# Clustered attention followed by a gated long convolution: TensorE's order written by hand, with routing and convolution units woven between attention steps

## The chip, the core and the metric

The kernel runs on one core of one Trainium2 chip. The metric is the device time of one execution in microseconds. Before the change the median of 2 runs is 709.45 us (708.78 to 710.13).

## The reference

```
q_assign = argmax(normalized q . normalized centroids)     # 16 clusters per head
k_assign = argmax(normalized k . normalized centroids)
scores = where(q_assign[q] == k_assign[k], q k^T / 8, -1e9)
attn = softmax(scores); x = attn v, heads side by side      # (4, 768, 512)
proj = x @ w_proj; x1, x2, x3 = the three 512-wide parts of proj
x2_conv = irfft(rfft(x2, axis=seq) * rfft(filter), axis=seq)
out = (x1 * x2_conv * x3) @ w_out
```

There are 4 batches, 8 heads, 768 positions, 64 channels a head; all inputs and the output are f32.

## The kernel before

The work is cut into eight *groups*, numbered from 0: four heads of one batch each, so that an even group and the odd one after it make a batch. A group has two *pairs* of heads, and a pair is worked off in six *steps*, one for each 128 keys.

`routing` (L248) finds the clusters of one group. Per pair and per Q or K it transposes six tiles on TensorE (L255), copies them out with ACT (L258), casts them with POOL into the operands `aug` (L260, L261) and multiplies with the normalised centroids (L264). The similarities are transposed back (L270), a chain on DVE (L274 to L282) makes one-hot rows, these are transposed (L286), scaled (`ohT`, L288) and written under Q and K in `aug` by eight DMAs on the SP queue (L293). So one matmul gives the score and the mask at once.

`attention` (L297) does one pair. A step has for each of the two heads two score matmuls in bf16 (L306) into a tile of two PSUM banks, an exp on ACT (L310) into one of eight f32 buffers `p`, and then four value matmuls in f32 (L314): for each half of the queries one for each head, the first head's into partitions 0 to 63 of the accumulator `o`, the second's into 64 to 127. DVE sums the exps into `acc` (L321). At the end of a pair, TensorE sums `acc` over the keys (four matmuls of 32 columns, L330); the denominators go through DRAM in a chain of DMAs on SP (`dd`, `dn`, `dr`, `rb`, L336 to L345); DVE scales the result (L348) and makes `uT` (L350, L351), POOL casts it to `xT` (L349).

`hyena` (L355) does the convolution of one batch after its two groups: the projection of x2 (L362), a transform along the sequence (`spectrum`, L230) with multiplications by the filter's spectrum (L370, L371), then for each of four *channel blocks* the projections x3 and x1 (L379), the inverse transform (L393) and the product (L402), and last the output projection (L409) and the store. `tables` (L156) makes the transform's matrices `fw` (L167 to L188), their transposes `inv` (L196, L199) and the filter's spectrum `hm` once at the start.

PSUM has eight banks: three tiles of two banks (`wide()`, L61) that scores, routing, convolution and tables share, and the accumulator `o` with two. The order of every engine's instructions comes from the language's scheduler, which goes by the program's order as a priority and by its own estimate of when an instruction is ready. The main loop (L425) traces the loads and the routing of group n+1, then attention of group n, then for odd groups the convolution.

Of the kernel before, what the change touches and what calls it, by code (L numbers as in the profile page):

```python
# [30 lines left out]
def kernel(  # L31
# [25 lines left out]
    psS = ctx.enter_context(tc.tile_pool(name="psS", bufs=3, space=PSUM))  # L57
    psO = ctx.enter_context(tc.tile_pool(name="psO", bufs=1, space=PSUM))
    dram = ctx.enter_context(tc.tile_pool(name="dram", bufs=2, space=bass.MemoryType.DRAM))

    def wide(nm="ps"):  # L61
        return psS.tile([128, 2, 512], F32, name="ps")
# [3 lines left out]
    vraw = ctx.enter_context(tc.tile_pool(name="vraw", bufs=2))  # L66

    def load_qk(b, g):
        qk = [[None] * 2 for _ in range(2)]
        for pr in range(2):  # L70
            for j, src in enumerate((q, k)):
                tl = qk[pr][j] = raw.tile([128, NT, 2, D], F32, name="qkraw")
                for hp in range(2):
                    nc.sync.dma_start(tl[:, :, hp], src[b, 4 * g + 2 * pr + hp].rearrange("(p t) d -> p t d", t=NT))
        return qk

    def load_v(b, g):
        vv = vraw.tile([128, 4, 384], F32, name="vraw")
        nc.sync.dma_start(vv, v[b, 4 * g:4 * g + 4].rearrange("h (p t) d -> p h (t d)", t=NT))
        return vv  # L80

    qk_raws = {(0, 0): load_qk(0, 0)}
    v_raws = {}

# [6 lines left out]
    nc.gpsimd.memset(ones32, 1.0)  # L91

# [11 lines left out]
    cbd = consts.tile([128, 4, 32], F32)  # L104
    nc.gpsimd.memset(cbd, 0.0)
    with tc.tile_pool(name="cen", bufs=1) as cen:
        c = cen.tile([128, D], F32)
        nc.scalar.dma_start(c, centroids.rearrange("h c d -> (h c) d"))
        c2 = cen.tile([128, D], F32)
        nc.vector.tensor_tensor(c2, c, c, op=Alu.mult)  # L110
        ss = cen.tile([128, 1], F32)
        nc.vector.tensor_reduce(ss, c2, axis=AX, op=Alu.add)
        nc.vector.tensor_scalar(ss, ss, 1e-30, None, op0=Alu.max)
        s0 = cen.tile([128, 1], F32)
        nc.scalar.activation(s0, ss, Act.Sqrt)

        s1 = cen.tile([128, 1], F32)
        nc.vector.reciprocal(s1, s0)
        nc.vector.tensor_tensor(s1, s1, ss, op=Alu.mult)
        nc.vector.tensor_tensor(s1, s1, s0, op=Alu.add)  # L120
        nc.vector.tensor_scalar(s1, s1, 0.5, 1e-6, op0=Alu.mult, op1=Alu.add)
        nc.vector.reciprocal(s1, s1)
        cn = cen.tile([128, D], F32)
        nc.vector.tensor_scalar(cn, c, s1, None, op0=Alu.mult)
        cps = wide()
        nc.tensor.transpose(cps[:D, 0, :128], cn, ident)
        cv = cps[:D, 0, :128].rearrange("d (r e c) -> d r e c", r=4, e=2)
        nc.vector.tensor_copy(cbd[:D, :, :NC], cv[:, :, 0])
        nc.vector.tensor_copy(cbd[D:, :, NC:], cv[:, :, 1])

# [11 lines left out]
    NP = 8  # L142
# [13 lines left out]
    def tables():  # L156
        with tc.tile_pool(name="tab", bufs=1) as tab, tc.tile_pool(name="tabw", bufs=2) as tabw:
            flo = tab.tile([128, 3, DM], F32)
            fhi = tab.tile([128, 3, DM], F32)
            fv = moe_filter_fft.rearrange("(w p m e) d -> w e p m d", w=2, p=64, m=3, e=2)  # L160
            for e in range(2):
                nc.sync.dma_start(flo[64 * e:64 * e + 64], fv[0, e])
                nc.sync.dma_start(fhi[64 * e:64 * e + 64], fv[1, e])
# [14 lines left out]
            for m in range(3):  # L178
                sm = tabw.tile([128, 1], F32)
                nc.vector.tensor_scalar(sm, s0, float(2 * m), None, op0=Alu.add)  # L180
                n = tabw.tile([128, 2, HS], F32)
                nc.vector.scalar_tensor_tensor(n, kc, sm, sh, op0=Alu.mult, op1=Alu.add)
                r = tabw.tile([128, 2, HS], F32)
# [5 lines left out]

            for j in range(6):  # L190
                tp = wide()[:].bitcast(BF16)
                for m in range(3):
                    cols = (0, 192, 0, 192, 128, 320)[j]
                    o = tp[:, 0, m * 128:(m + 1) * 128]
                    if j < 4:
                        nc.tensor.transpose(o, fw[j // 2][:, m, cols:cols + 128], identb)  # L196
                    else:
                        for i in range(2):
                            nc.tensor.transpose(o[64 * i:64 * i + 64], fw[i][:, m, cols:cols + 64], identb)  # L199
                nc.scalar.copy(inv[:, j], tp[:, 0, :HS])  # L200
# [14 lines left out]
            for i in range(3):  # L215
                ps = spectrum(i, fu, fd)
                if i == 0:
                    nc.vector.tensor_scalar(hm[:, 0, 0], ps[:, 0], wv, None, op0=Alu.mult)
                    nc.vector.tensor_scalar(hm[:, 0, 2], ps[:, 1], wz, None, op0=Alu.mult)
                    d1 = tab.tile([128, DM], F32)  # L220
                    nc.vector.tensor_scalar(d1, ps[:, 1], w1, None, op0=Alu.mult)
                    nc.vector.scalar_tensor_tensor(hm[:, 0, 3], ps[:, 0], wz, d1,
                                                   op0=Alu.mult, op1=Alu.add)
                else:
                    nc.vector.tensor_scalar(hm[:, i, 0], ps[:, 0], 2.0 / S, None, op0=Alu.mult)
                    nc.vector.tensor_scalar(hm[:, i, 2], ps[:, 1], 2.0 / S, None, op0=Alu.mult)
                    nc.vector.tensor_scalar(hm[:, i, 3], ps[:, 0], 2.0 / S, None, op0=Alu.mult)
                nc.vector.tensor_scalar(hm[:, i, 1], hm[:, i, 2], -1.0, None, op0=Alu.mult)

    def spectrum(i, fu, fd):  # L230

        ps = wide()
        for cs in range(2):
            for m in range(3):
                if i < 2:
                    nc.tensor.matmul(ps[:, cs], fw[i][:, m, 192 * cs:192 * cs + 128], (fu, fd)[i][:, m],  # L236
                                     start=(m == 0), stop=(m == 2))
                else:
                    for e in range(2):
                        nc.tensor.matmul(ps[64 * e:64 * e + 64, cs],  # L240
                                         fw[e][:, m, 192 * cs + 128:192 * cs + 192], (fu, fd)[e][:, m],
                                         start=(m == 0), stop=(m == 2))
        return ps
# [4 lines left out]
    def routing(b, g, aset):  # L248
        qk = qk_raws.pop((b, g))
        sim_ps = wide()  # L250
        for pr in range(2):
            for j in range(2):
                tps = wide()
                for t in range(NT):
                    nc.tensor.transpose(tps[:, t // 3, (t % 3) * 128:(t % 3) * 128 + 128],  # L255
                                        qk[pr][j][:, t].rearrange("p h d -> p (h d)"), ident)
                qkT = rt.tile([128, 2, 384], F32, name="qkT", bufs=2)
                nc.scalar.copy(qkT, tps[:, :, :384])  # L258
# [166 lines left out]
    for n, (b, g) in enumerate(groups):  # L425
# [11 lines left out]
        if g == 1:  # L437
            hyena(b, xT, uT)
# [30 lines left out]
```

## Time and profile before

| | |
|---|---|
| median of 2 runs | 709.45 us |
| profiled execution | 709.35 us |
| its span | 707.6 us |
| PE (TensorE) busy | 549.3 us, 78% |
| DVE busy | 319.4 us, 45% |
| ACT busy | 255.5 us, 36% |
| POOL busy | 140.2 us, 20% |
| mean granted TensorE clock | 0.921 |

The busy times are of one core; PEld is the load of weights, which overlaps PE. Matmuls are pipelined, so that the duration of one record is longer than the distance to the next, and the distance between starts is the cost. In the timeline's rows the first number is the start in us from the span's start, the second the length; "x2" are records merged into one row; in brackets stands the idle time of the engine before the row, and what ended it. L-numbers are lines of the kernel before.

### The profile page before, as it was taken

How to read it: one execution, taken by the hardware profiler on the slowest of the kernel's cores; microseconds unless marked ns; L12 is line 12 of the kernel's file. 1: busy time of each engine (PE TensorE's matmuls, PEld its weight loads, DVE VectorE, ACT ScalarE, POOL GpSimd, SP SyncE). 2: the span in 40 equal slices, each digit the busy share in tenths (PEclk: the TensorE clock that was granted, in tenths of full speed). 3: DMA queues.
4: the chain of work that ended last, by engine and by line, in shares of the span. 5: the costliest groups of instructions: out<-in, count | busy, mean ns of one | idle time of the engine just before them, and what ended most of it. 6: DMA issues, size and time to landing. Idle time of an engine off the chain costs nothing.

```text
span 707.6 us, 6740 instructions
## 1 busy us (share of the span) xinstructions
PE 549.3 (78%) x2408; PEld 203.1 (29%) x2417; DVE 319.4 (45%) x403; ACT 255.5 (36%) x352; POOL 140.2 (20%) x170
## 2 busy tenths in 40 slices
PE   4266996995787899699387699699487699998574
PEld 2122222321333223222133222332133332222232
DVE  3663453653540543546162356364353144565251
ACT  2133452452223354354114254255122345553122
POOL 6402004000434002100063200400044300000062
PEclk9768999898899899899799899899889989999799
DMA  9943014203006003302102400510200200000002
GB/s 203 193 110 78 7 24 102 67 2 90 1 0 179 12 2 105 84 3 60 32 1 98 90 3 24 125 44 22 70 1 1 89 12 2 24 23 25 23 1 89
DMA packets 67539, 37.48 MB, mean 53 GB/s; under 512 B 56945, under 2 KB 62641, under 8 KB 67505
## 3 DMA queue, kind: packets, MB, share of 16 engines
q1 hardware_dynamic: 66304, 34.91, 19.7%
q0 software_dynamic: 1056, 2.10, 1.7%
q8 instruction: 19, 0.31, 0.2%
q14 instruction: 16, 0.12, 0.1%
q10 hardware_dynamic: 144, 0.03, 0.0%
HBM read 31.06 MB, written 6.49 MB: 53 GB/s over the span
## 4 chain that ended last, share of the span: by engine, by line
PE 61%; DVE 14%; ACT 8%; POOL 7%; DMA 6%; issue 3%; SPq 1%; POOLq 0%; ACTq 0%; DVEq 0%
PE o L314 30%; PE ps L306 11%; PE ps L264 6%; POOL hy L402 4%; PE ps L362 3%; POOL hy L371 3%; PE ps L255 3%; PE ps L330 3%; DVE tm L370 2%; DMA rb<-dr 2%; ACT qkT L258 2%; PE ps L409 2%; DMA dd<-den 1%; DVE cand L276 1%; DVE yy L400 1%
## 5 line engine op out<-in xcount | busy, mean ns | idle before, releaser
L362 PE MATMUL ps<-wpj,uT 128*128 128x512 bf16 x92 | 28.9, 471 | 44.8 <-DVE uT L350 44.6
L379 PE MATMUL ps<-xT,wpj 128*128 128x384 bf16 x256 | 45.6, 326 | 12.9 <-ACT x_3066 L382 1.3
L274 DVE TENSOR_REDUCE mx<-ps 128x48 f32<-128x768 f32 x8 | 7.7, 958 | 105.0 <-PE ps L270 105.0
L264 PE MATMUL ps<-qkT,cbd 128*32 128x384 f32 x128 | 44.7, 503 | 10.1 <-ACT qkT L258 9.1
L314 PE MATMUL o<-p_156,vraw 128*64 128x384 f32 (+1 forms) x96 | 45.8, 575 | 0.2 <-ACT p_156 L310 0.2
L314 PE MATMUL o<-p_160,vraw 128*64 128x384 f32 (+1 forms) x96 | 41.3, 512 | 2.0 <-ACT p_160 L310 2.0
L314 PE MATMUL o<-p_158,vraw 128*64 128x384 f32 (+1 forms) x96 | 41.3, 512 | 1.5 <-ACT p_158 L310 1.5
L258 ACT COPY qkT<-ps 128x768 f32<-128x768 f32 x32 | 24.9, 800 | 48.3 <-PE ps L255 48.3
L314 PE MATMUL o<-p_162,vraw 128*64 128x384 f32 (+1 forms) x96 | 41.3, 512 | 0.0
L370 DVE TENSOR_TENSOR tm<-ps,hm 128x1024 f32<-128x1024 f32 x24 | 29.0, 1223 | 26.8 <-PE ps L236 25.1
L310 ACT ACTIVATE p_156<-ps 128x768 f32<-128x768 f32 x24 | 19.5, 811 | 54.6 <-PE ps L306 54.6
L314 PE MATMUL o<-p_157,vraw 128*64 128x384 f32 (+1 forms) x96 | 39.1, 534 | 0.0
L314 PE MATMUL o<-p_159,vraw 128*64 128x384 f32 (+1 forms) x96 | 36.2, 499 | 0.5 <-ACT p_159 L310 0.5
L371 POOL TENSOR_TENSOR hy<-tm 128x512 bf16<-128x512 f32 x24 | 30.0, 1270 | 32.8 <-DVE tm L370 32.0
L314 PE MATMUL o<-p_161,vraw 128*64 128x384 f32 (+1 forms) x96 | 36.2, 499 | 0.0
L314 PE MATMUL o<-p_163,vraw 128*64 128x384 f32 (+1 forms) x96 | 36.1, 499 | 0.0
L286 PE MATMUL ps<-identb,oh 128*128 128x128 bf16 x48 | 6.6, 310 | 36.9 <-DVE oh L282 36.9
L364 ACT CAST hy<-ps 128x1024 bf16<-128x1024 f32 x12 | 12.1, 1012 | 63.3 <-PE ps L362 63.1
L379 PEld LDWEIGHTS <-wpj 128*128 128x128 bf16 x256 | 24.0, 97 | 33.2 <-issue 16.6
L260 POOL CAST aug_132<-qkT 64x768 bf16<-64x768 f32 x4 | 3.3, 821 | 152.5 <-ACT qkT L258 152.5
L409 PE MATMUL ps<-wout,hy 128*128 128x512 bf16 x92 | 23.2, 379 | 8.9 <-POOL hy L402 4.2
L310 ACT ACTIVATE p_163<-ps 128x768 f32<-128x768 f32 x24 | 19.5, 811 | 29.3 <-PE ps L306 29.3
(518 smaller groups left out, 1033.6 us busy)
## 6 DMA issues: line engine op xcount, KB each, us to landing
qkraw<-in_q_dram SPq DMA_DIRECT2D x32, 192.0 KB
qkraw<-in_k_dram SPq DMA_DIRECT2D x32, 192.0 KB
vraw<-in_v_dram SPq DMA_DIRECT2D x8, 768.0 KB
rb<-dr SPq DMA_DIRECT2D x32, 192.0 KB
out_dram<-tm SPq DMA_DIRECT2D x12, 512.0 KB
wpj<-in_moe_w_proj_dram POOLq DMA_DIRECT2D x1, 1536.0 KB, 12.0
dd<-den SPq DMA_DIRECT2D x64, 1.5 KB
flo<-in_moe_filter_fft_dram SPq DMA_DIRECT2D x2, 384.0 KB
```

Of the source, the lines that this page charges most:

```text
L255: nc.tensor.transpose(tps[:, t // 3, (t % 3) * 128:(t % 3) * 128 + 128], qk[pr][j][:, t].rearrange("p h d -> p (h d)"), ident)
L258: nc.scalar.copy(qkT, tps[:, :, :384])
L264: nc.tensor.matmul(sim_ps[32 * z:32 * z + 32, ch, :384], cbd[:, 2 * g + pr], qkT[:, ch], start=True, stop=True)
L306: nc.tensor.matmul(sps[:, ch, :384], augs[aset][pr][hp][1][:K, ts(sk, 128)], augs[aset][pr][hp][0][:K, ts(ch, 384)], start=True, stop=True)
L310: nc.scalar.activation(pb[hp][sk][:, :S].rearrange("p (a b) -> p a b", a=2), sps[:, :, :384], Act.Exp, scale=0.125)
L314: nc.tensor.matmul(o[64 * hp:64 * hp + 64, ch, :384 + ch], vv[:, 2 * pr + hp, sk * D:(sk + 1) * D], pb[hp][sk][:, 384 * ch:384 * ch + 384 ...
L362: nc.tensor.matmul(ps[:, e], uvf[:, e, kt, ts(m, 128)], wpj[:, kt, DM:2 * DM], start=(kt == 0), stop=(kt == ND - 1))
L370: nc.vector.tensor_tensor(tm, ps, hm[:, i, 2 * r:2 * r + 2], op=Alu.mult)
L371: nc.gpsimd.tensor_tensor(y[:, i, r], tm[:, 0], tm[:, 1], op=Alu.add)
L379: nc.tensor.matmul(ps[:, ch, :384], wpj[:, kt, off + dt * 128:off + dt * 128 + 128], xT[:, kt, ts(ch, 384)], start=(kt == 0), stop=(kt == ...
L402: nc.gpsimd.tensor_tensor(y2[:, dt], yy[:].rearrange("p t c -> p (t c)"), x3[:].rearrange("p a b -> p (a b)"), op=Alu.mult)
L409: nc.tensor.matmul(ps[:, e], y2[:, kt, ts(2 * tt + e, 128)], wout[:, kt], start=(kt == 0), stop=(kt == ND - 1))
```

## The change

The scheduler no longer orders TensorE: from the first routing on its instructions are issued in the order in which the program traces them (`tc.manual_schedule` for PE). The other engines and the DMA queues are ordered as before.

PSUM is divided anew: two tiles of two banks for scores alone, two single banks (`bank()`) for all else, and two for `o`.

Routing, tables and convolution are rewritten as generators. Each `yield` ends a *unit* that writes one bank: three transposes, the four similarity matmuls of one half, four projection matmuls, and so on. Routing has 17 units with three empty ones in it, the convolution 42. The convolution's inverse transform takes both banks. Copies out of PSUM, the filter multiplications and the gate are cut to one bank each; `x3` has two buffers, `qkT` four, `p` six in place of eight.

The main loop walks through all 96 steps. In step i it issues the scores of step i+1 of the first head, half of the units due, the scores of the second head, the other half, then at the start of a new pair the denominators of the last one (`finish`), and then the four value matmuls of step i. Twelve steps make a group. The units in a group come from the routing of the next group and, from the fourth step of an even group that is not the first, from half of the convolution of the batch before; the odd group's list has the other half. `emit` takes the next unit of the generator with the largest share left. At the first step of each group the generators of the old list are drained. What is left in the last step is issued ahead of that step's scores. The first routing and the tables, and the last convolution, are drained in one piece.

Also: the sine tables (`forward_tables`) come ahead of the first routing, the Q and K loads of a group follow one by one the transposes that free their buffers, V is loaded at the first step of the group before, the denominators go out in one DMA in place of four, and the second routing is woven into group 0.

```diff
-    psS = ctx.enter_context(tc.tile_pool(name="psS", bufs=3, space=PSUM))
+    psS = ctx.enter_context(tc.tile_pool(name="psS", bufs=2, space=PSUM))
     psO = ctx.enter_context(tc.tile_pool(name="psO", bufs=1, space=PSUM))
+    psF = ctx.enter_context(tc.tile_pool(name="psF", bufs=2, space=PSUM))
...
+    def bank():
+        return psF.tile([128, 512], F32, name="pf")
...
-    NP = 8
+    NP = 6
...
+    def routing(n):
+        aset, g = n % NSET, n % 2
+        qkT = {}
         for pr in range(2):
             for j in range(2):
+                qr = qk_raws.pop((n, pr, j))
+                z = 2 * pr + j
+                qkT[z] = rt.tile([128, 2, 384], F32, name="qkT", bufs=4)
+                for ch in range(2):
+                    tps = bank()
+                    for t in range(3):
+                        nc.tensor.transpose(tps[:, ts(t, 128)],
+                                            qr[:, 3 * ch + t].rearrange("p h d -> p (h d)"), ident)
+                    nc.scalar.copy(qkT[z][:, ch], tps[:, :384])
+                    if ch == 1:
+                        load_qk(n + 1, pr, j)
+                    yield
...
+        for ch in range(2):
+            sim_ps = bank()
+            for z in range(4):
+                nc.tensor.matmul(sim_ps[32 * z:32 * z + 32, :384], cbd[:, 2 * g + z // 2],
+                                 qkT[z][:, ch], start=True, stop=True)
+            nc.scalar.copy(sim[:, ch], sim_ps[:, :384])
+            yield
...
+        for _ in range(3):
+            yield
...
+        def values(self, sk):
...
             for ch in range(2):
                 for hp in range(2):
-                    nc.tensor.matmul(o[64 * hp:64 * hp + 64, ch, :384 + ch],
-                                     vv[:, 2 * pr + hp, sk * D:(sk + 1) * D],
+                    nc.tensor.matmul(self.o[64 * hp:64 * hp + 64, ch, :384 + ch],
+                                     vv[:, 2 * self.pr + hp, sk * D:(sk + 1) * D],
...
-        for z in range(4):
-            nc.sync.dma_start(dd[z:z + 1], den[32 * z:32 * z + 1])
+            nc.sync.dma_start(dd, den[0:128:32])
...
+            x3 = hw.tile([128, 2, 384], F32, name="x3", bufs=2)
+            for ch in range(2):
+                for off in (2 * DM, 0):
+                    ps = bank()
                     for kt in range(ND):
...
+                    if off:
+                        nc.scalar.copy(x3[:, ch], ps[:, :384])
+                    else:
+                        nc.vector.tensor_tensor(x3[:, ch], ps[:, :384], x3[:, ch], op=Alu.mult)
+                    yield
+            po, pe = bank(), bank()
...
+    NR, NH, NTAB = 17, 42, 12
+    forward_tables()
+    ctx.enter_context(tc.manual_schedule(engines={mybir.EngineType.PE}))
...
+    def emit(k):
+        for _ in range(k):
+
+            live = [f for f in fill if f[1] > 0]
+            if not live:
+                return
+            f = max(live, key=lambda f: f[1] / f[2])
+            f[1] -= 1
+            next(f[0], None)
...
+    for i, (n, pr, sk) in enumerate(steps):
+        w = i % 12
+        if w == 0:
+            for f in fill:
+                drain(f[0])
+            fill = []
+            if n + 1 < len(groups):
+                fill.append([routing(n + 1), NR, NR])
+            if groups[n][1] == 1 and hq:
+                fill.append([hq[0], NH - NH // 2, NH - NH // 2])
+            if 0 < n < len(groups) - 1:
+                load_v(*groups[n + 1])
+        if w == 3 and groups[n][1] == 0 and n > 0:
+            b = groups[n][0] - 1
+            hq = [hyena(b, *xu[b])]
+            fill.append([hq[0], NH // 2, NH // 2])
+        left = sum(f[1] for f in fill)
+        nf = -(-left // (12 - w)) if left else 0
+        if i % 12 == 11:
+
+            emit(left)
+            nf = 0
+        scores(i + 1, 0)
+        emit((nf + 1) // 2)
+        scores(i + 1, 1)
+        emit(nf // 2)
+        if sk == 0 and i:
+            pairs[steps[i - 1][:2]].finish()
+        pairs[n, pr].values(sk)
+    pairs[steps[-1][:2]].finish()
+    drain(hyena(B - 1, *xu[B - 1]))
```

391 lines of the change are left out of this document (197 added, 194 removed).

## The prediction

> **What bounds the kernel now.** I read the page first, then TensorE's timeline, and from it cut the span into stages and asked for the busy time of each. The columns of the second fence: start and end, length, busy time of PE, PEld, DVE, ACT and POOL with the number of instructions, the granted clock, DMA share and GB/s.
>
> ```profile
> span 707.6 us, 6740 instructions
> PE 549.3 (78%) x2408; PEld 203.1 (29%) x2417; DVE 319.4 (45%) x403; ACT 255.5 (36%) x352; POOL 140.2 (20%) x170
> ```
>
> ```profile
> 49.40:66.46 17.06, 9.75 (x52) 5.16 (x53) 8.31 (x13) 5.18 (x6) 6.59 (x8) 0.90 0.41 92
> 66.46:108.30 41.84, 41.59 (x162) 12.08 (x160) 21.78 (x26) 20.86 (x29) 0.00 (x0) 0.96 0.07 15
> 108.30:125.10 16.80, 10.06 (x55) 5.24 (x53) 4.70 (x8) 4.55 (x7) 7.37 (x9) 0.88 0.50 121
> 165.90:216.70 50.80, 32.67 (x169) 14.76 (x169) 18.79 (x24) 10.37 (x15) 16.45 (x12) 0.90 0.08 24
> 649.40:707.60 58.20, 34.52 (x173) 14.99 (x174) 19.82 (x26) 12.17 (x17) 17.17 (x12) 0.89 0.10 35
> ```
>
> The stages follow one another: tables and two routings until the first score at 66.46, attention of a group (41.84, PE busy 41.59), a routing (16.80, PE busy 10.06), attention, the convolution of a batch (50.80, PE busy 32.67), and so on; 649.40 to the end is the last convolution with the chain ahead of it. Check: 66.5 + 8 x 41.3 + 6 x 16.8 + 3 x 50.8 + 58.2 = 708. So attention is bound by TensorE, and TensorE idles in routing and convolution, where it waits for DVE, ACT, POOL and DMA.
>
> Inside attention, one step (one block of 128 keys of a pair of heads) on TensorE:
>
> ```profile
> 72.76 0.50 PE L306 MATMUL ps<-aug_132,aug_133 80*128 80x384 bf16 x2
> ...
> 73.19 0.54 PE L314 MATMUL o<-p_159,vraw 128*64 128x384 f32 x1
> ...
> 73.19 0.54 PE L314 MATMUL o<-p_158,vraw 128*64 128x385 f32 x1
> ...
> 73.29 0.81 ACT L310 ACTIVATE p_160<-ps 128x768 f32<-128x768 f32 x1 [0.41 <-PE ps L306]
> 73.56 0.49 PE L314 MATMUL o<-p_159,vraw 128*64 128x384 f32 x1
> ...
> 73.57 0.49 PE L314 MATMUL o<-p_158,vraw 128*64 128x385 f32 x1
> 73.88 0.81 PE L314 MATMUL o<-p_159,vraw 128*64 128x385 f32 x2
> ...
> 74.14 0.96 DVE L321 TENSOR_TENSOR acc_537<-acc_537,p_160 128x768 f32<-128x768 f32 x1 [0.26 <-ACT p_160 L310]
> 74.62 0.50 PE L306 MATMUL ps<-aug_134,aug_135 128*128 128x384 bf16 x2
> ...
> 75.05 0.86 PE L314 MATMUL o<-p_160,vraw 128*64 128x384 f32 x2
> ...
> 75.85 0.50 PE L306 MATMUL ps<-aug_132,aug_133 80*128 80x384 bf16 x2
> ```
>
> From 72.76 to 75.85 the step takes 3.09 us. Each f32 value matmul is two records. Those of the two heads write different halves of the columns (128*64), and where two such matmuls are neighbours they run at once: both first records start at 73.19, both second ones at 73.56/73.57. But a score pair stands between the first value matmul (75.05, alone, 0.80 to the next) and the other three, of which the last (73.88, 0.74) is alone too.
>
> **The change, part by part.** All sums are against the profiled execution, 709.35 us or 1.75 over its span, and 0.1 under the median of the runs.
>
> *Steps.* By hand, a step is scores, units, scores, units and then all four value matmuls together. Neighbours pair: two pairs of two slots, 1.43 us (the length from 73.19 to 74.62, also four slots) in place of 0.80 + 1.43. Scores stay 2 x 0.43 (72.76 to 73.19). Step: 2.29 us. The trace shows no first pair of this kind, whose two outputs share a bank; the nearest row that does share one is in the sums of the denominators:
>
> ```profile
> 85.10 0.83 PE L330 MATMUL ps<-acc_537,ones_91 128*32 128x384 f32 x2
> ...
> 87.30 0.51 PE L330 MATMUL ps<-acc_537,ones_91 128*32 128x384 f32 x1
> 87.31 0.52 PE L330 MATMUL ps<-acc_538,ones_91 128*32 128x384 f32 x2
> ...
> 88.08 0.50 PE L306 MATMUL ps<-aug_136,aug_137 80*128 80x384 bf16 x2
> ```
>
> One of four, cut off by a value matmul, takes 0.83 alone; the other three, in one bank, start within 0.01 and are over after 0.78 (87.30 to 88.08). So I take the pairing. Put together, all four cost 0.78, not 1.6. A group becomes 12 x 2.29 + 2 x 0.78 = 29.0; eight: 232. ACT needs 2 x 0.81 and DVE 2 x 0.96 of the 2.29, so TensorE still sets the pace, DVE close behind.
>
> *Routing.* Seven of the eight move into the steps.
>
> ```profile
> 113.39 1.48 PE L264 MATMUL ps<-qkT,cbd 128*32 128x384 f32 x4 [0.29 <-ACT qkT L258]
> 114.80 0.87 PE L255 MATMUL ps<-ident,qkraw 128*128 128x128 f32 x6
> 115.61 2.51 PE L264 MATMUL ps<-qkT,cbd 128*32 128x384 f32 x8
> ...
> 124.50 0.82 PE L286 MATMUL ps<-identb,oh 128*128 128x128 bf16 x6 [4.62 <-DVE oh L282]
> ```
>
> 24 transposes cost 4 x 0.81 (114.80 to 115.61). The similarities, today 1.48 for each of the first two tiles and 2.5 for the rest, are put so that the four column groups of a half stand together: two slots of 0.37 a half, 1.5 in all. Six transposes of the similarities at 0.81, six of the one-hots at 0.82: 6.35 us, seven times 44. The 4.62 wait for DVE goes: three empty units, four steps, lie over it.
>
> *Convolution.* At full clock its matmuls are 32.67 x 0.90 = 29.4 us; three woven: 88. But only half is woven. At the first step of each group every generator in the list is drained, and the half-done convolution is among them: its remaining units (a bit over two of four channel blocks and the output projection) come as one block at the start of the odd group, and the odd group's slots are then empty. What a block pays:
>
> ```profile
> 202.40 1.81 POOL L402 TENSOR_TENSOR hy<-yy,x_1226 128x768 bf16<-128x768 f32 x1 [2.83 <-DVE yy L401]
> ...
> 207.03 1.81 POOL L402 TENSOR_TENSOR hy<-yy,x_1262 128x768 bf16<-128x768 f32 x1 [2.83 <-DVE yy L401]
> ...
> 211.67 1.80 POOL L402 TENSOR_TENSOR hy<-yy,x_1298 128x768 bf16<-128x768 f32 x1 [2.83 <-DVE yy L401]
> ...
> 213.53 3.41 PE L409 MATMUL ps<-wout,hy 128*128 128x512 bf16 x15 [1.06 <-POOL hy L402]
> ```
>
> A channel block takes 4.63 (202.40 to 207.03) for 24 matmuls of about 0.16 (half a 0.32 slot), 4.0. With two single banks in place of three double ones I put it at 5.4, since the inverse transform needs both at once and waits for the evictions of two: 1.4 more, twice. The projection then waits for the last product, 1.8 on POOL with DVE and ACT ahead of it, about 3.5. Together 6.5 a batch (bounds 5 and 8): 20.
>
> *New waits.* TensorE's order is now fixed, so whatever waits there holds all behind it. First, the convolution begins three steps after the denominators of the last pair are issued.
>
> ```profile
> 649.83 0.49 PE L330 MATMUL ps<-acc_3639,ones_91 128*32 128x384 f32 x1
> ...
> 650.89 1.13 SPq L336 DMA_DIRECT2D dd<-den  x4
> ...
> 662.43 5.81 PE L362 MATMUL ps<-wpj,uT 128*128 128x512 bf16 x15 [10.05 <-DVE uT L350]
> ```
>
> That chain (four DMA hops) takes 12.6; one issue in place of four (1.13) saves 0.8. Its cover is one set of values, two steps with two short units each and a score pair, 1.4 + 2 x 3.1 + 0.4 = 8. The loads of V and of the next Q and K are now on SP in the same steps, so I take 6 us of wait, three times: 18 (bounds 9 and 30). Behind it wait all scores, so ACT and DVE too.
>
> Second, the one-hot rows of the next group reach its operands late.
>
> ```profile
> 66.71 0.68 DVE L288 TENSOR_SCALAR ohT<-ps,mka,mkb 128x768 bf16<-128x768 bf16 x1 [0.92 <-PE ps L286]
> 67.42 0.58 SPq L293 DMA_DIRECT2D aug_140<-ohT  x1
> ...
> 68.71 0.58 SPq L293 DMA_DIRECT2D aug_141<-ohT  x1
> ```
>
> Today a whole group lies between. By the new order the one-hot transposes are the last routing unit but one, in the step before the last, and the next group's first scores open the last step. Those need the first and third of eight DMAs: 0.7 (DVE), 0.2, 1.9 (two issues and the third's own), a landing of about 1.6 (estimate: a hop of the chain above is about 2.4 with its issue) and some queueing on DVE: 5. The cover is 1.4 to 2.7. Wait 3, seven times: 21 (bounds 10 and 28).
>
> Third, each unit writes one of two banks. Some 217 units with matmuls are woven or in blocks; a bank comes back after an ACT or DVE instruction queued among exps (0.81) and sums (0.96). No row shows this. Bounds: 0, and 0.3 a unit; I take 0.15, 32 us, which is to cover DVE's queue as well.
>
> *Start.* The second routing (17.06) leaves it. The forward tables move ahead of the first routing:
>
> ```profile
> 37.31 0.40 PE L196 MATMUL ps<-identb,fw_174 128*128 128x128 bf16 x2 [8.83 <-ACT fw_174 L188]
> ...
> 41.55 0.39 PE L196 MATMUL ps<-identb,fw_174 128*128 128x128 bf16 x2 [2.67 <-ACT fw_174 L188]
> ```
>
> Those waits, 11.5, are the most that is to be had. The filter's load now comes after group 1's Q, K and V in the program and may have to wait for the memory of the tables' scratch, so I take 5 (bounds 0 and 11.5). First score at 66.5 - 17.1 - 5 = 44.4.
>
> *End.* The last convolution has nothing to hide in: 58.2, less 0.8, plus 3 x 0.8 for its channel blocks (4.63 to 5.4), plus about 2 as fewer matmuls are done ahead of each wait: 62.
>
> Sum: 44.4 + 232 + 44 + 88 + 20 + 18 + 21 + 32 + 62 = 561; with 1.75, 563 us.
>
> **Rivals.**
> 1. *No pairing* in the new places (values 2.2 us as now, sums 1.6, similarities 5.2): 96 x 0.8 + 16 x 0.8 + 7 x 3.7 = 116 more, 679. Against it stand the rows at 73.19 and 87.30.
> 2. *DVE sets the pace.* A batch needs 2 x (21.78 + 4.70) + 18.79 = 72 us of DVE against 2 x 35.4 + 29.4 = 100 of TensorE, enough room unless POOL slows it. POOL has 2 x 7.37 + 16.45 = 31 a batch, which today lies mostly outside attention. Where they meet:
>
> ```profile
> 108.00 0.55 DVE L351 TENSOR_TENSOR uT<-x_645 128x384 bf16<-128x384 f32 x1
> ...
> 179.33 1.18 DVE L351 TENSOR_TENSOR uT<-x_1089 128x384 bf16<-128x384 f32 x1
> ```
>
> The same instruction takes 0.55 alone and 1.18 beside a POOL cast. If half of POOL's 31 is added to DVE, the peaks no longer fit, some 45 us over three batches: 608. [...]
> 3. *The clock falls.* Attention ran at 0.96, the stages with many short waits at 0.88 to 0.90. If the weave brings those waits everywhere, 364 us of TensorE work at 0.89: 29 more, 592. [...]
> 4. *Slower: the two banks.* If ACT's order puts both exps of a step (1.6 us) ahead of a unit's copy, a unit waits about 1 us for its bank: 217 x 1.0 in place of 32: 748. From 0.9 a unit the kernel is over 2% slower, from 0.8 it is level. Against it: ACT is 36% busy, and the unit's own length and the score pair lie over most of an exp.
>
> **How the numbers follow.** Forecast 0.64 (own range 525 to 605: all waits at their lower bounds would give about 495, all at their upper 625, and not all go one way); no pairing 0.07; DVE 0.14; clock 0.06; two banks 0.09, of which 0.04 lands level. Likeliest: 563. 520 to 630 leaves out the no-pairing case, the two banks and a few in 100 below. A measurement of this kernel can tell 2% from no change (695 to 724): faster 0.91, same 0.04, slower 0.05.
>
> **What would show it.** Steps without units at 2.3 us, with the four value matmuls in four slots; no TensorE stage without scores but for the start, three blocks of some 20 us at the start of the fourth, sixth and eighth group, and the end; TensorE waiting for uT three times and for the one-hot DMAs seven times; the first score near 44. Wrong would be: steps at 3 us (rival 1), a DVE without gaps (2), TensorE waiting for copies ahead of most units (4).

## The result and the profile after

The changed kernel takes 574.76 us (573.53 to 575.99, 2 runs) against 709.45: a ratio of 0.810, 95% interval 0.802 to 0.818. The forecast was 563, with a range of 520 to 630. The profiled execution took 573.53 us, 1.8 over its span. L-numbers from here on are those of the kernel after or, under an experiment, those of its own kernel, unless another one is named. One execution of experiment 7, at 557.0 us with a granted clock of 0.919 where the other three had 0.926 to 0.936, counts as slow and is left out of its numbers.

The page's first lines, after (busy us, share of the span, number of instructions):

```profile
span 571.7 us, 6805 instructions
PE 432.3 (76%) x2405; PEld 179.9 (31%) x2417; DVE 339.7 (59%) x459; ACT 257.6 (45%) x432; POOL 177.1 (31%) x168
```

TensorE's busy time fell from 549.3 to 432.3 us: 117 of the 136 us of the span are matmul time that is no longer spent, not waits that were filled. The span cut into stages (start, the eight groups, the end; the columns as in the prediction: start and end, length, PE, PEld, DVE, ACT, POOL, the granted clock, DMA share, GB/s):

```profile
0.00:53.84 53.84, 16.59 (x100) 9.19 (x102) 27.71 (x48) 13.93 (x26) 20.12 (x56) 0.71 0.71 161
53.84:88.06 34.22, 31.20 (x198) 13.60 (x197) 28.44 (x35) 23.21 (x37) 10.85 (x8) 1.00 0.26 62
88.06:124.72 36.66, 33.51 (x212) 14.10 (x213) 31.62 (x39) 24.46 (x40) 12.92 (x10) 1.00 0.37 93
124.72:192.48 67.76, 53.20 (x294) 21.97 (x297) 45.95 (x58) 30.58 (x51) 23.26 (x18) 0.90 0.20 50
...
451.34:508.20 56.86, 49.91 (x251) 18.53 (x252) 26.85 (x38) 27.42 (x43) 6.25 (x4) 0.91 0.12 42
508.20:571.70 63.50, 37.17 (x176) 15.20 (x176) 21.70 (x36) 14.07 (x27) 17.14 (x12) 0.89 0.09 35
```

The eight groups take 454.4 us (508.20 - 53.84), where the prediction's terms between the first score and the end add to 455. The first score is at 53.84, not at 44.4, and that is nearly the whole miss. The end takes 63.5 for 62.

A step with no unit in it, TensorE's timeline:

```profile
76.41 0.50 PE L325 MATMUL ps<-aug_140,aug_141 80*128 80x384 bf16 x2
76.74 0.49 PE L325 MATMUL ps<-aug_142,aug_143 128*128 128x384 bf16 x2
77.16 0.54 PE L340 MATMUL o<-p_162,vraw 128*64 128x384 f32 x1
77.17 0.54 PE L340 MATMUL o<-p_163,vraw 128*64 128x384 f32 x1
...
78.18 0.49 PE L340 MATMUL o<-p_162,vraw 128*64 128x385 f32 x1
78.19 0.49 PE L340 MATMUL o<-p_163,vraw 128*64 128x385 f32 x1
78.61 0.50 PE L325 MATMUL ps<-aug_140,aug_141 80*128 80x384 bf16 x2
```

From 76.41 to 78.61 it takes 2.20 us, against 3.09 before. The value matmuls of the two heads start 0.01 us apart, the last pair at 78.18/78.19, so that eight records fill four slots.

What TensorE waited for (us in total, times, longest):

```profile
PE pf L391 <- DVE uT L379: 32.1, 5, 8.4
PE pf L301 <- DVE oh L295: 14.6, 2, 13.7
PE pf L240 <- DVE fu L208: 14.5, 1, 14.5
PE ps L325 <- DMA aug_137<-ohT: 9.8, 3, 3.7
PE ps L325 <- DMA aug_145<-ohT: 9.4, 4, 2.5
```

The first row has two waits of the end in it (2.30 and 8.39); the other three, 21.4 us, are those ahead of a woven convolution. The one-hot DMAs are the fourth and fifth row, seven waits, 19.2 us. The third row and 13.7 us of the second belong to the start.

### The profile page after: what moved, and what is told of

It reads as the page before. It is cut to its first block, busy times and chain, and to the rows that moved or that the text cites. A ratio compares the mean times of both kernels' runs of the same rounds, so it can differ in the third digit from the quotient of the medians.

```text
span 571.7 us, 6805 instructions
## 1 busy us (share of the span) xinstructions
PE 432.3 (76%) x2405; PEld 179.9 (31%) x2417; DVE 339.7 (59%) x459; ACT 257.6 (45%) x432; POOL 177.1 (31%) x168
## 4 chain that ended last, share of the span: by engine, by line
PE 45%; DVE 25%; DMA 10%; issue 8%; SPq 5%; ACT 5%; POOL 2%; POOLq 0%; DVEq 0%; ACTq 0%
PE o L340 15%; PE ps L325 8%; PE pf L391 5%; PE pf L447 4%; DMA rb<-dr 4%; PE pf L412 3%; DVE tm L401 3%; SPq L308 3%; PE pf L262 2%; PE pf L275 2%; PE pf L359 2%; DMA dr<-dn 2%; PE pf L428 2%; DVE uT L380 2%; DMA fhi<-in_moe_filter_fft_dram 1%
## 5 line engine op out<-in xcount | busy, mean ns | idle before, releaser
L329 ACT ACTIVATE p_160<-ps 128x768 f32<-128x768 f32 x32 | 26.0, 812 | 76.1 <-PE ps L325 71.0
L412 PE MATMUL pf<-xT,wpj 128*128 128x384 bf16 x256 | 50.7, 326 | 12.7 <-ACT od L431 5.7
L340 PE MATMUL o<-p_165,vraw 128*64 128x385 f32 (+1 forms) x128 | 55.0, 558 | 0.0
L340 PE MATMUL o<-p_164,vraw 128*64 128x385 f32 (+1 forms) x128 | 55.0, 558 | 0.0
L391 PE MATMUL pf<-wpj,uT 128*128 128x512 bf16 x92 | 30.4, 476 | 32.4 <-DVE uT L379 32.1
L340 PE MATMUL o<-p_161,vraw 128*64 128x385 f32 (+1 forms) x128 | 48.2, 499 | 0.0
L340 PE MATMUL o<-p_163,vraw 128*64 128x385 f32 (+1 forms) x128 | 48.2, 499 | 0.0
L340 PE MATMUL o<-p_160,vraw 128*64 128x385 f32 (+1 forms) x128 | 48.2, 499 | 0.0
L340 PE MATMUL o<-p_162,vraw 128*64 128x385 f32 (+1 forms) x128 | 48.2, 499 | 0.0
L404 POOL TENSOR_TENSOR hy<-tm 128x512 bf16<-128x512 f32 x24 | 32.1, 1360 | 50.1 <-DVE tm L401 50.1
L401 DVE TENSOR_TENSOR tm<-pf,hm 128x512 f32<-128x512 f32 x48 | 30.0, 682 | 18.4 <-PE pf L240 11.3
L329 ACT ACTIVATE p_164<-ps 128x768 f32<-128x768 f32 x32 | 26.0, 812 | 31.9 <-PE ps L325 31.9
L412 PEld LDWEIGHTS <-wpj 128*128 128x128 bf16 x256 | 23.6, 97 | 40.6 <-issue 21.1
L447 PE MATMUL pf<-wout,hy 128*128 128x512 bf16 x92 | 26.4, 438 | 11.4 <-POOL hy L437 8.8
L262 PE MATMUL pf<-ident,qkraw 128*128 128x128 f32 x192 | 33.0, 286 | 1.0 <-ACT qkT L264 0.8
L264 ACT COPY qkT<-pf 128x384 f32<-128x384 f32 x64 | 30.9, 486 | 4.8 <-PE pf L262 4.8
L329 ACT ACTIVATE p_162<-ps 128x768 f32<-128x768 f32 x32 | 26.2, 818 | 14.1 <-PE ps L325 14.1
L262 PEld LDWEIGHTS pf<-ident,qkraw 128*128 128x128 f32 x192 | 25.4, 147 | 8.3 <-ACT qkT L264 2.8
L428 PE MATMUL pf<-inv,hy 128*128 128x384 bf16 (+1 forms) x128 | 22.0, 326 | 7.2 <-DVE x_1550 L417 0.6
L329 ACT ACTIVATE p_163<-ps 128x768 f32<-128x768 f32 x32 | 26.4, 824 | 1.8 <-PE ps L325 1.4
L329 ACT ACTIVATE p_161<-ps 128x768 f32<-128x768 f32 x32 | 26.1, 816 | 0.6 <-PE ps L325 0.2
```

Source lines behind the costliest of these rows:

```text
L262: nc.tensor.transpose(tps[:, ts(t, 128)], qr[:, 3 * ch + t].rearrange("p h d -> p (h d)"), ident)
L264: nc.scalar.copy(qkT[z][:, ch], tps[:, :384])
L329: nc.scalar.activation(p[:, :S].rearrange("p (a b) -> p a b", a=2), sps[:, :, :384], Act.Exp, scale=0.125)
L340: nc.tensor.matmul(self.o[64 * hp:64 * hp + 64, ch, :384 + ch], vv[:, 2 * self.pr + hp, sk * D:(sk + 1) * D], pb[hp][sk][:, 384 * ch:384 * ...
L391: nc.tensor.matmul(ps, uvf[:, e, kt, ts(m, 128)], wpj[:, kt, DM:2 * DM], start=(kt == 0), stop=(kt == ND - 1))
L401: nc.vector.tensor_tensor(tm[r][:, cs], ps, hm[:, i, 2 * r + cs], op=Alu.mult)
```

## The experiments

Each kernel was compared with the kernel before on its own chip; the median of before was 709 to 711 us in all of them. One theory runs through them: TensorE sets the time, so that a change is worth what it takes from TensorE's matmuls and waits. The rivals say that an edit is worth nothing because another engine or wait is close behind.

**1. Is it neighbourhood that pairs the value matmuls?** The two matmuls of a head are issued one behind the other:

```diff
-            for ch in range(2):
-                for hp in range(2):
+            for hp in range(2):
+                for ch in range(2):
```

> After the change, but the four value matmuls of a step go head by head (first head both halves, then second head both halves), so that only the middle two are neighbours of different column halves. Theory (the pairing of neighbours carries the gain in the steps): a step has six slots of 0.32 to 0.37 in place of four, 0.65 us more, 96 times: 62 us, so about 637 us; a step without units takes 2.85 in place of 2.20. Rival (the order inside the values does not matter, the gain is the weave's): within 2% of 575.

Measured: 575.5 us (573.1 to 579.8), ratio 0.810 (0.806 to 0.815), the same as the changed kernel. The step in this kernel's timeline:

```profile
78.38 0.82 PE L325 MATMUL ps<-aug,aug 80*128 80x384 bf16 x4
79.14 1.52 PE L340 MATMUL o<-p,vraw 128*64 128x384 f32 x8
80.59 0.66 PE L325 MATMUL ps<-aug,aug 80*128 80x384 bf16 x3
```

The eight records still take four slots (79.14 to 80.59, 1.45 us) and the step 2.20 (78.38 to 80.59). The expectation fell, and with it my word "neighbours". Since the first two matmuls of this order write the same half of the columns, I read the four slots so that the third issued ran beside the first and did not wait for the second; the row merges the eight records, so this is worked out from their 1.45 us. The weight loads of the step fit it, four at 79.14, two at 79.51 and two at 79.84.

**2. What, then, parts them?** The second head's scores, which take all 128 columns (128*128 in the rows below), are put between the first value matmul and the other three, as the order of the kernel before had them:

```diff
-        def values(self, sk):
+        def values(self, sk, between):
...
+                    if ch == 0 and hp == 0:
+                        between()
...
-        scores(i + 1, 1)
...
-        pairs[n, pr].values(sk)
+        pairs[n, pr].values(sk, lambda: scores(i + 1, 1))
```

> After the change, but the second score pair of a step is issued between the first value matmul and the other three, as it stood before; all else stays. Theory (value matmuls into different column halves run at once unless a matmul over all columns stands between them, whatever their order): the first one is alone again (0.8 us), so is the last (0.7), a step without units takes about 3.0 us in place of 2.20, and 96 times 0.75 make 72: about 647 us. Rival (the steps are shorter because the scores of the next step are issued ahead, so that no exp is waited for): within 2% of 575.

Measured: 631.5 us (628.2 to 632.7), ratio 0.889 (0.886 to 0.892). The step with one unit of transposes in it:

```profile
74.52 0.50 PE L325 MATMUL ps<-aug,aug 80*128 80x384 bf16 x2
74.86 0.49 PE L284 MATMUL pf<-ident,sim 128*128 128x128 f32 x3
75.28 0.86 PE L340 MATMUL o<-p,vraw 128*64 128x384 f32 x2
76.07 0.50 PE L325 MATMUL ps<-aug,aug 128*128 128x384 bf16 x2
76.50 1.51 PE L340 MATMUL o<-p,vraw 128*64 128x384 f32 x6
77.94 0.50 PE L325 MATMUL ps<-aug,aug 80*128 80x384 bf16 x2
```

The first matmul is alone again, 75.28 to 76.07, and the other three take four slots: 3.42 us with the unit, some 3.09 without (the unit adds 0.33), 0.89 more than 2.20. That is 85 us over 96 steps, but the kernel lost only 57: the longer steps cover waits. TensorE's waits for the one-hot DMAs, for instance, are 5.2 us here and 19.2 in the changed kernel, and the mean granted clock is 0.935 here and 0.910 there.

The full width may not be the only thing that parts. In the kernel before, right behind the sum of a denominator over 32 columns that the prediction shows at 85.10, stands:

```profile
85.87 0.54 PE L314 MATMUL o<-p_159,vraw 128*64 128x384 f32 x1
```

This value matmul writes the other half of the columns (64 to 127, the sum 0 to 31), and the exp that it needs ended at 85.29, but it started only 0.77 after the sum's start, when the sum's two records (0.83 together) were all but over. So two matmuls of different column widths did not run at once here, though they write different columns. Whether it is the full width in between that parts, or any change of the width, is not told apart.

**3. What is the weave worth?** Nothing is woven: a group's routing is one block at its first step, the convolution one block at the fourth step of the next even group.

```diff
-                fill.append([routing(n + 1), NR, NR])
+                drain(routing(n + 1))
...
-            hq = [hyena(b, *xu[b])]
-            fill.append([hq[0], NH // 2, NH // 2])
+            drain(hyena(b, *xu[b]))
```

> After the change, but nothing is woven: the routing of the next group is issued as one block at the first step of a group, the convolution of the batch before as one block at the fourth step of an even group; the order of the value matmuls stays. Theory (the pairing carries most of the 135 us, the weave the smaller part): seven routings as blocks cost 14.5 us each in place of 6.4 woven, but the wait of 2.8 for the one-hot DMAs goes: 38 us more; the first half of three convolutions 9 us more each: 27. About 640 us. Rival (the weave carries the gain): 690 or more, near the kernel before.

Measured: 611.1 us (610.6 to 612.6), ratio 0.860 (0.857 to 0.864). The weave is worth 36 us, half of what I expected. One block of routing in this kernel:

```profile
95.70 0.88 PE L262 MATMUL pf<-ident,qkraw 128*128 128x128 f32 x6
...
100.63 1.50 PE L275 MATMUL pf<-qkT,cbd 128*32 128x384 f32 x16 [0.24 <-ACT qkT L264]
102.08 1.19 PE L284 MATMUL pf<-ident,sim 128*128 128x128 f32 x6
108.01 0.82 PE L301 MATMUL pf<-identb,oh 128*128 128x128 bf16 x6 [4.74 <-DVE oh L295]
108.62 1.49 PE L325 MATMUL ps<-aug,aug 80*128 80x384 bf16 x4
```

The block takes 12.9 us (95.70 to 108.62) where a routing took 16.8 before: the similarities are 1.45 us in one place, not the 5.2 of before. A block is dearer than units (4.74 us of waiting for DVE, 1.3 us for the copies), but the cheaper matmuls are there without any weaving.

**4. Both edits in one kernel**, blocks and scores between:

> Nothing woven, and the second pair of scores issued between the first value matmul and the other three: the two edits that were measured apart (611 and 631 us) in one kernel. Theory (the loss of the pairing is PE time of the step itself, 0.59 us in each of 96 steps, whatever else is woven): 611 plus 57, which is 668 us, between 660 and 676; the rest of the way to 709 is then neither the weave nor the pairing. Rival (without woven units ScalarE's exponentials set the step, so that PE has room): 611 to 640 us.

Measured: 691.0 us (690.1 to 692.1), ratio 0.973 (0.970 to 0.976): 80 us more than the blocks alone, above both expectations. The step here is that of the kernel before, 3.09 us:

```profile
125.93 0.50 PE L325 MATMUL ps<-aug,aug 80*128 80x384 bf16 x2
...
129.02 0.50 PE L325 MATMUL ps<-aug,aug 80*128 80x384 bf16 x2
```

So the way from 709 to 575 can be walked in three legs: about 18 us for everything else (709 to 691: the start and cheaper blocks among it, not told apart), 80 for the four value matmuls in one place (691 to 611), 36 for the weave (611 to 575). Going from the other end, the pairing counts 57 in the woven kernel, because there the slower steps hide waits.

**5. The start.** The filter gets memory of its own and is loaded ahead of the sine tables and the first routing:

```diff
-            flo = tab.tile([128, 3, DM], F32)
-            fhi = tab.tile([128, 3, DM], F32)
...
+    flt = flts.enter_context(tc.tile_pool(name="flt", bufs=1))
+    flo = flt.tile([128, 3, DM], F32)
+    fhi = flt.tile([128, 3, DM], F32)
...
     forward_tables()
```

> After the change, but the filter is loaded into memory of its own ahead of the first routing, where its load does not wait for the scratch of the sine tables. Theory (the start is late by the 14.5 us that TensorE waits for the sum of the filter's halves): the sum then begins when DVE is done with the tables near 29, the first score comes near 40 in place of 53.8, total about 561 us. Rival (DMA bandwidth holds the start: the bytes ahead of the first score are the same, so Q, K and V of the groups 0 and 1 come later): the first score within 4 us of 53.8, total 571 to 576.

Measured: 558.7 us (555.1 to 560.2), ratio 0.785 (0.781 to 0.789), 16 less; the first score is at 40.0, and the wait for `fu` is gone. What held the load in the changed kernel is on the timelines of ScalarE, the SP queue and DVE:

```profile
29.26 0.51 ACT L182 ACTIVATE fw_175<-n 128x384 bf16<-128x384 f32 x1
...
29.55 0.61 SPq L308 DMA_DIRECT2D aug_136<-ohT  x1
...
34.07 0.54 SPq L308 DMA_DIRECT2D aug_143<-ohT  x1
34.72 0.59 SPq L191 DMA_DIRECT2D flo<-in_moe_filter_fft_dram  x1
...
44.79 1.76 DVE L208 TENSOR_TENSOR fu<-flo,fhi 128x1536 bf16<-128x1536 f32 x1 [15.27 <-DMA fhi<-in_moe_filter_fft_dram]
```

The four DMAs of the load are queued right behind the eight one-hot DMAs of the first routing, so that this place in the queue holds the load from 29.55 to 34.72. The memory, which the load takes over from the scratch of the sine tables, is read for the last time until 29.77 (the first row). From the load's first issue to DVE's sum of the halves it is another 10 us (34.72 to 44.79). So the place in the queue alone is worth at most some 5 of the 14.5 us (an estimate from these rows); the rest is the load's own way, which could not begin before the memory was free. The experiment takes both away.

**6. The block of the odd groups.** The convolution that is half done stays in the list:

```diff
-                drain(f[0])
+                if not (groups[n][1] == 1 and hq and f[0] is hq[0]):
+                    drain(f[0])
```

> After the change, but at the first step of an odd group the half-done convolution is not drained, so that its second half is woven as the list has it. Theory (the block of about 22 us at the start of the groups 3, 5 and 7 holds 14 us of TensorE work): 7 to 8 us less three times, about 552 us, and no stage without scores between the start and the end. Rival (DVE sets the pace where units are woven, so the waits only move into the steps): within 2% of 575.

Measured: 556.4 us (556.0 to 556.6), ratio 0.783 (0.780 to 0.785), 18 less, 6 a batch. This kernel leaves out one store, that of the last third of batch 2.

**7. The wait for uT.** The convolution's first units come at the seventh step:

```diff
-        if w == 3 and groups[n][1] == 0 and n > 0:
+        if w == 6 and groups[n][1] == 0 and n > 0:
```

> After the change, but the convolution's units come from the seventh step of an even group on in place of the fourth, more of them in a step. Theory (TensorE waits 8, 8 and 6 us for uT because the chain over DRAM is longer than three steps): three more steps of 3 us lie over it, the waits go, 15 to 18 us less, about 558 us. Rival (the denser units then wait for DVE and the banks): within 1% of 575.

Measured: 548.5 us (547.2 to 552.2), ratio 0.774 (0.770 to 0.777), 26 less, more than expected. The waits for uT fell from 32.1 to 10.9, which are those of the end: 21.2 us of waits, and 5 us more than that in time. TensorE's busy time fell as well, with the same matmuls, from 432.3 to 424.2 us; the mean granted clock is 0.933 here and 0.910 in the changed kernel, and the slower clock behind such waits (0.50 over the next 4 us, below under Clock) fits that.

**8. The one-hot DMAs.** All units are issued within ten steps of a group:

```diff
-        nf = -(-left // (12 - w)) if left else 0
+        nf = -(-left // max(1, 10 - w)) if left else 0
```

> After the change, but the units of a group are spread over its first ten steps in place of twelve. Theory (TensorE waits about 2.8 us at the end of seven groups for the DMAs of the one-hot rows, which start too late): two steps of 2.2 us without units then lie over them, so these 19 us go but for 1 to 3, about 558 us. Rival (the chain is longer in truth, as the SP queue is busy with other DMAs): half of it, 565.

Measured: 558.5 us (557.1 to 559.8), ratio 0.787 (0.784 to 0.789), 16 less. TensorE no longer waits for these DMAs anywhere; its waits for uT grew from 32.1 to 36.3 and those for `x` ahead of the inverse transform (L428) from some 7 to 13.4; so the gain is a little less than the 19.2 us of waits removed.

**9. VectorE beside POOL.** The routing's casts move from POOL to ScalarE:

```diff
-                nc.gpsimd.tensor_copy(augs[aset][pr][0][j][:D], qf[:D])
-                nc.gpsimd.tensor_copy(augs[aset][pr][1][j][D:], qf[D:])
+                nc.scalar.copy(augs[aset][pr][0][j][:D], qf[:D])
+                nc.scalar.copy(augs[aset][pr][1][j][D:], qf[D:])
```

> After the change, but the casts of Q and K into the operands of the scores run on ACT in place of POOL (64 of about 0.8 us). Theory (DVE has room, its sums are slowed beside POOL's casts but nobody waits for them): the sums of the exps take 0.96 each again, and the time stays within 1% of 575. Rival (DVE, slowed by POOL, sets the pace of the woven steps): 3% less or better, 558. A third case, ACT too full with 51 us more: above 580.

Measured: 577.6 us (574.5 to 579.4), ratio 0.814 (0.812 to 0.817). The busy times on this kernel's page:

```profile
PE 434.5 (76%) x2405; PEld 180.0 (31%) x2417; DVE 322.8 (56%) x459; ACT 309.4 (54%) x496; POOL 91.0 (16%) x104
```

DVE's work got 17 us shorter (339.7 to 322.8) with the same instructions, so POOL's casts did slow it, and the time stayed. DVE did not set the pace.

**10. The four repairs together** (5 to 8, with the convolution's units cut 15 to 27 and what is left drained at the end):

```diff
...
-                drain(f[0])
+                if not (groups[n][1] == 1 and hq and f[0] is hq[0]):
+                    drain(f[0])
...
-                fill.append([hq[0], NH - NH // 2, NH - NH // 2])
+                fill.append([hq[0], NH - 15, NH - 15])
...
-        if w == 3 and groups[n][1] == 0 and n > 0:
+        if w == 6 and groups[n][1] == 0 and n > 0:
...
-            fill.append([hq[0], NH // 2, NH // 2])
+            fill.append([hq[0], 15, 15])
...
-        nf = -(-left // (12 - w)) if left else 0
+        nf = -(-left // max(1, 10 - w)) if left else 0
...
+    for f in fill:
+        drain(f[0])
```

> Four repairs in one kernel, the output complete: the filter loaded early, the second half of a convolution woven with no block (what is left of it drained after the last step), the convolution from the seventh step of an even group with 15 units there and 27 in the odd group, and every unit issued within ten steps. Theory (each repair takes away a wait of PE of its own, so that they add up): 575 less 16, 18, 24 and 16, which is 501 us, between 495 and 515; the block of an odd group's start is gone, the wait for uT in the loop is under 10 us in sum. Rival (with the waits of PE gone VectorE or ScalarE sets the pace, as their work stays the same): the gains overlap and the time is 520 to 545 us, and PE's waits for p, tm and od grow in place of those removed.

Measured: 515.8 us (514.0 to 516.6), ratio 0.726 (0.724 to 0.729): just outside the theory's range, and faster than the rival's. It is the fastest kernel together with the next, which can't be told from it. The stretch between first and last score, and the waits:

```profile
39.20:445.70 406.50, 363.67 (x2117) 151.82 (x2128) 306.46 (x376) 228.53 (x378) 145.76 (x101) 0.97 0.25 68
```

```profile
PE pf L384 <- DVE uT L372: 16.5, 3, 10.8
PE pf L405 <- DVE x L410: 12.2, 5, 3.6
```

The parts alone save 77 us, together 59. Of the first row 10.8 us are at the end, so that the waits for uT in the loop are 5.7. TensorE is busy for 89% of this stretch (363.67 of 406.50), and a new wait stands in the list, for the gate `x` that DVE makes: 12.2 us ahead of the projections, in 5 pieces, three of them 3.6 long. What DVE does ahead of the first of these:

```profile
153.99 2.02 DVE L370 SCALAR_TENSOR_TENSOR x<-osb,rb 128x768 f32<-128x768 f32 x1
...
156.80 1.17 DVE L372 TENSOR_TENSOR uT<-x 128x384 bf16<-128x384 f32 x1
...
158.37 0.54 DVE L410 TENSOR_TENSOR x<-pf,x 128x384 f32<-128x384 f32 x1
...
158.96 0.81 PE L405 MATMUL pf<-xT,wpj 128*128 128x384 bf16 x4 [3.60 <-DVE x L410]
```

The gate's projection is over at 154.70, but DVE first does the end of a pair: the scaling, a sum of exps (0.94) and the two parts of `uT`, without a pause from 153.99 to the gate at 158.37. The other two waits of 3.6 stand behind the same four instructions. So here it is the order of DVE's own work that TensorE waits for. No run puts the gate ahead of that work.

**11. The repairs, and the casts on ScalarE** (the edits of 9 and 10):

> The four repairs together (515.8 us) and the casts of the routing on ScalarE instead of POOL. Theory (with TensorE's waits gone, VectorE's sums of 1.12 to 1.37 us beside POOL's casts are what is late now, so that the same edit that was worth nothing on the changed kernel is worth something here): TensorE's waits for x, 22 us in sum, fall by half and the time is 500 to 508 us. Rival (VectorE's place is only taken by ScalarE, whose copies come later): 512 to 525 us, with the waits for qkT and od longer.

Measured: 516.8 us (514.0 to 518.0), ratio 0.727 (0.724 to 0.730): the rival. DVE's busy time fell from 356.4 to 332.4 us, but TensorE's waits for `x` ahead of the projections only from 12.2 to 10.8, three times 3.6, behind the same four instructions of DVE. Those for `qkT` grew from 3.8 to 10.8; those for `od`, which the rival named too, did not grow. The routing's casts on POOL are therefore not what makes `x` late.

## Why the prediction was right, and where not

**Steps and pairing.** Right in size, 2.20 against 2.29, and eight groups of 12 steps and two finishes (0.78 each, as forecast) take 224 us, not 232. The rival of no pairing (679) fell; what it stood for is worth 57 to 80 us. But the reason was wrong in one point: "neighbours pair" (experiment 1). What counts is that no matmul over the full width stands between (experiment 2, some 3.09 us a step with one between and 2.20 with none; by the one row at 85.87 another column width may part as well). Routing was cheaper too: three transposes take 0.33, not 0.41.

**Waits.** uT: forecast 6 us three times, 18 in sum; measured 8.0, 7.9 and 5.6, 21.4. One-hot DMAs: forecast 3 us seven times, 21; measured 2.3 to 3.7, 19.2. Both are where the prediction put them, and experiments 7 and 8 show that they count: 26 us for 21.2 removed, and 16 for 19.2, with other waits grown.

**Blocks and banks.** There are three blocks of 22 to 25 us at the start of the fourth, sixth and eighth group. A channel block of the first of them, and the output projection of the first and of the third, TensorE's timeline:

```profile
197.11 0.33 PE L428 MATMUL pf<-inv,hy 128*128 128x384 bf16 x1
...
202.99 0.33 PE L428 MATMUL pf<-inv,hy 128*128 128x384 bf16 x1
...
214.42 4.71 PE L447 MATMUL pf<-wout,hy 128*128 128x512 bf16 x21 [2.19 <-POOL hy L437]
...
473.74 7.56 PE L447 MATMUL pf<-wout,hy 128*128 128x512 bf16 x21 [2.19 <-POOL hy L437]
```

The channel block takes 5.88 (197.11 to 202.99), where I took 5.4. The 6.5 us a batch that I gave to the blocks agree with the 6 that experiment 6 gained. The hand-over of banks was too dear at 32 (12 of the 217 units are empty ones of the convolution, which makes less than 2 us of it). TensorE's idle time in the eight groups is 454.4 less its busy 378.5, that is 76; less the two waits above (40.6) 35 are left for hand-over and blocks together, where the ledger had 52. The rival of two banks (748) fell with it.

**Clock.** The term that the ledger lacked. It counted TensorE's work at full clock. The granted clock in the eight groups, weighted by busy time, is 0.94 (378.5 us of busy time, 355 at full clock), some 23 us at most, since a group's mean also counts the slow clock that falls into its waits. Where it goes: the first 4 us after waits, and in the last two rows the output projections of the first and the third block:

```profile
88.06:92.00 3.94, 3.80 (x22) 1.77 (x22) 2.04 (x3) 3.01 (x6) 1.07 (x1) 1.00 0.25 45
124.72:128.70 3.98, 3.98 (x14) 1.31 (x15) 2.49 (x3) 1.64 (x3) 1.22 (x1) 0.59 0.10 25
147.63:151.60 3.97, 3.97 (x10) 1.49 (x11) 1.11 (x2) 1.98 (x3) 0.63 (x1) 0.50 0.00 0
214.42:222.00 7.58, 7.13 (x41) 3.45 (x43) 0.16 (x1) 5.77 (x11) 0.02 (x1) 1.00 0.52 208
473.70:481.50 7.80, 7.76 (x24) 2.95 (x25) 0.00 (x0) 3.10 (x6) 0.00 (x0) 0.62 0.24 98
```

After a one-hot wait of 2.5 us at 124.72, and after the uT wait of 8 us at 147.63, TensorE works the next 4 us at 0.5 to 0.6: it pays for a wait a second time, with about 1.7 us for a one-hot wait and 2 for a uT wait (estimates: the missing share of the clock times the busy time). The same windows behind all ten waits of the two kinds show it nine times (the one at 88.06 left the clock at 1.00), 16 us in sum. The two output projections stand behind the same wait of 2.19 us: the first kept the clock and took 4.71 for its 21 matmuls, the third lost it (0.62) and took 7.56; the second block's kept it too. So the lower clock does cost time, and the length of the wait alone does not decide. The third rival's price of 29 is 364 us at 0.89 against the 0.96 of attention; against the full clock of the ledger it would have been 45. So half of the third rival came true, by another way than the woven steps: groups 0 and 1, which write two banks in turn like the others but have no wait for uT and no block, ran at 1.00, and with the waits repaired the loop ran at 0.97 (experiment 10). The clock fell behind four of the five waits of 2.3 to 2.5 us in the groups, and behind one of the three of 2.19.

**The sum.** Within the groups the misses cancel: steps, routing and hand-over 30 us too dear, the clock some 23 too cheap, waits and convolution the rest. A forecast of 455 for 454.4 is therefore less exact than it looks.

**Start.** The step that failed is "so I take 5 (bounds 0 and 11.5)" and its 44.4. It saw that the filter's load might wait for memory, but costed only the gain of earlier tables and not the loss: the load now stands behind eight one-hot DMAs on SP, and TensorE waits 14.5 us for `fu`. A row of the kernel before showed 0.58 for one such issue; eight of them are 5 us that I left out. With the load out of the way the first score comes at 40.0 (experiment 5), so that the gain that I counted was there to be had. The queue's order took at most some 5 us of the wait; the rest is the load's own 10 us, which began only after the sine tables were done with the memory, and the 44.4 has no term for that.

**DVE.** The second rival's mechanism is there (17 us less DVE work without the routing's casts on POOL), but its price was not: 0 in the changed kernel and 0 in the repaired one. DVE's busy time fell with the edit in both (339.7 to 322.8, and 356.4 to 332.4 us), and the time did not follow.

## What to carry to other kernels

Matmuls that use half of the array's columns ran beside those of the other half here as long as nothing over the full width was issued between them (a step of 2.20 us, against 3.09 with a score pair between); by one row (85.87) another column width may keep them apart as well. Putting them in one place was worth more (57 to 80 us) than the weave as first written (36), and about as much as the weave with its waits repaired (611 to 516, of which 16 are the start). In an order written by hand a wait in front of TensorE cost its length and often the clock behind it here (0.50 to 0.61 over the next 4 us after nine of ten waits), so look for the two or three long ones first and move their consumers a few steps later. When work is moved ahead in the program, read what the same queue holds in front of it.

## What was not expected of the hardware

- The two column halves did not need to be fed in turn: with the order first half, first half, second half, second half, eight records still filled four slots of 0.36 us (1.45 us in sum). The step took 2.20 us, where I had expected 2.85.
- After a wait of 2.3 to 3.7 us TensorE's granted clock was 0.50 to 0.61 over the next 4 us in six of seven cases, and 1.00 in the seventh.
- Slower steps were partly free: the same 0.89 us a step cost 80 us where nothing was woven, and 57 where waits stood behind it.
